# One fused transformer layer on one core: Gelu rebuilt from tanh tile by tile, a reordered prologue, zero products in TensorE's gaps, and a new step table

## The chip, the core and the metric

The kernel runs on one core of one Trainium2 chip. The core has five engines that run their own instruction lists side by side: TensorE (PE in the profile, with its weight loads as PEld), VectorE (DVE), ScalarE (ACT), GpSimd (POOL) and SyncE (SP, which here only issues transfers). They meet through semaphores. The metric is the device time of one execution in microseconds; lower is better. The time before is the median of three executions, 686.83 us (685.43 to 691.41).

## The reference

The input x has 2048 rows of 512 in bf16. It is layer-normalised, and the normalised rows feed two branches whose results are added to x:

```python
xn = _layernorm(x)
return x + A(xn, wqkv, wo) + B(xn, w1, b1, w2, b2)

# A: attention with 32 heads of 16
qkv = xn @ wqkv;  p = softmax(q k^T * 16 ** -0.5);  A = (p v) @ wo
# B: a second layernorm, then an MLP along the 2048 rows ("token mixing"), 1376 hidden
h = _layernorm(xn)
u = gelu(h^T @ w1 + b1)          # approximate=True, the tanh form; 512 x 1376
B = (u @ w2 + b2)^T
```

The tanh form of Gelu is 0.5 u (1 + tanh(0.798 (u + 0.0447 u^3))).

## The kernel before, in words

**The attention.** Scores are made transposed, 128 keys by 512 queries for one head: a *tile*. There are 32 heads x 16 key blocks x 4 query blocks = 2048 of them. They are worked off in 32 *blocks* of 4 heads x 16 key blocks, and `pos()` counts in blocks. Four heads' score products (`score_mm`, L621) run as four row strips of PE's array, each into one of seven PSUM banks. A bank is emptied in one of two ways:

- ACT takes the exponential (`exp_tile`, L634) of one, two or three neighbouring banks into the ring `pT`. One product with V (`pv_mm`, L647) uses each tile.
- DVE makes an approximate exponential with integers (`dve_first`, L667): the bits of an int16 read as bf16. Its error is evened out by two more copies, shifted by a constant, which POOL (an integer add, L676) or DVE (L678) makes four tiles at a time (`make_plane`). Three products with V then use each such tile. The copies live in `planes` and, once they are free, in `x_sb` and `xn_sb`.

The eighth bank gathers the product with V for one block; DVE copies it out (L1057), and the row sums go through DRAM and come back as factors for L1100.

**The MLP.** For each of 11 blocks of hidden columns, 16 product groups accumulate h^T w1 in a bank (`chain_ut`), DVE adds the bias into `gT` (L953), and after the eleventh block one call, `gelu_all`, runs Gelu on ACT: one instruction over ten blocks (L931), one over the last (L934). From then on 16 chains `chain_yo` make the products with w2, add wo's and the residual (`xres`) and store through `osb`. The hidden blocks are planned for positions 4.4 to 15.28 and the output chains from 15.68 on (`ut` and `yo` in L60).

**The order of work.** Nothing is ordered by the hardware: a planner in Python runs when the kernel is built. It keeps a clock for each engine, a cost for each operation and, for each engine in turn, picks the next instruction; each engine's list is then fixed, with waits where an operand comes from another engine. The engines run their lists in order. `pe_step` chooses among score products, PV products, a step of an MLP or projection chain, and, when nothing fits, `z_fill` (L1553): four products of zeros added to the PV bank. It does so until position 5 (`z_to`), and only where ACT has enough work queued. [...] `burst` chooses how many of the next four tiles go to DVE; the balance between ACT and DVE, the width of ACT's instructions and much else are parameters, and the table `STEP_VALUES` (L66) sets them anew at each of 32 positions.

**The prologue** (L457 to L716) is written out by hand. The loads: SP issues x tile 0, 1, 2, 3, then the weights of v, then the rest of x; ACT issues the first weights of q and k, and loads the table set that has both ln and exp. PE runs 8 zero products (L682), then for each of four tiles of x: statistics (DVE, L493), one over the deviation (two small ACT steps, L500 and L502), normalisation (DVE, L507), transpose (PE, L546), copy (ACT or DVE), projection to q (L534). Tile 0 of k follows, and after the fourth tile the first masked q (L587) and the first exponential.

Of the kernel before, what the change touches and what calls it, by code (L numbers as in the profile page):

```python
# [41 lines left out]
def _plane_sum(i):  # L42
    tot = 0.0
    for d, w in zip(SHIFT, WEIGHT):
# [10 lines left out]
N_ZERO0 = 8  # L55
N_ZERO1 = 2
NXP = 5
# [4 lines left out]
            pl_open=3, f_bias=0.0, f_early=9.0, s_wait=-1e9, tol2=-1e9, ex2=2.0, ex3=1.0, d_from=1.3, z_to=5.0, partial=False, pr_ex=0, dve_planes=6,  # L62
            v1=lambda a: (1.2 + 0.8 * a / 16.0, 0.6), v2=lambda a: (2.4 + 1.3 * a / 16.0, 1.6),
            kt=lambda T, c: ((0, 1.0, 2.9, 4.6)[T] + 0.17 * c * (1, 1, 2, 2)[T], (0, 0.5, 2.0, 3.2)[T]))
STEP_KEYS = ("bal", "bal_w", "d_from", "d_keep", "d_last", "d_slack", "d_stop", "dve_planes", "early", "ex2", "ex3", "f_bias", "f_early", "f_items", "f_late", "f_pr", "lk", "lone", "lone_n", "marg", "one_first", "open_pl", "partial", "pl_next", "pl_open", "pr_ex", "q_max", "ring_low", "ring_next", "tol", "trip")
STEP_VALUES = (  # L66
# [32 lines left out]
)  # L99
STEPS = [dict(zip(STEP_KEYS, v)) for v in STEP_VALUES]  # L100
HOOK = [None]
SCORE = (1.05, 0.5, 0.3)
CP_EVERY = 64
NU = 16
NQS = 4
NW1 = 2
NW2 = 2


# [1711 lines left out]
```

## Time and profile before

| | us |
|---|---|
| median of three executions | 686.83 |
| the profiled execution | 684.76 |
| its span, first to last instruction | 683.0 |
| ACT busy | 664.8 |
| PE busy (modelled ends) | 655.6 |
| DVE busy | 567.9 |
| POOL busy | 493.7 |
| first exponential starts | 12.97 |
| Gelu on ACT, with its two table loads | 341.04 to 348.64 |

Rows of groups read: line, engine, operation, out<-in, count, then busy us, mean ns of one, and the idle time of the engine just before them with what ended it. In a timeline row the first two numbers are start and length in us, and a bracket gives the idle time before. Windows give busy time for each engine, with the granted clock of PE (1.00 is full).

### The profile page before, as it was taken

To read this page: it belongs to the slowest core of one execution; us is meant where nothing else is said; L and a number is where in the kernel's file an instruction comes from. 1 tells how busy PE (TensorE), PEld (TensorE's weight loads), DVE (VectorE), ACT (ScalarE), POOL (GpSimd) and SP (SyncE) were. 2 spreads that over 40 slices of the span, in tenths; PEclk is the share of its full clock that TensorE was granted. 3 is DMA by queue.
4 is the path that set the end of the run, shared out by engine and by line. 5 is a ranking of instruction groups with operands and counts; after the bars stand their busy time and mean duration, and the time that the engine had idled before them with its cause. 6 is when DMAs were issued, how large, how long until landed. Compare 5 with 4: busy or idle time off the path is not lost.

```text
span 683.0 us, 20375 instructions
## 1 busy us (share of the span) xinstructions
PE 655.6 (96%) x8596; PEld 205.4 (30%) x8597; DVE 567.9 (83%) x939; ACT 664.8 (97%) x822; POOL 493.7 (72%) x515
## 2 busy tenths in 40 slices
PE   7899999999999999999989999999999999999996
PEld 3433333332222233323322222222323222222222
DVE  7888978779778798888958898788888899887794
ACT  5999999999999999999999999999999999999995
POOL 2409888767766679766678666669989699788783
PEclk9999999999999999999999999999999999999999
DMA  7050100112122021210021012121221211111101
GB/s 217 22 125 11 27 4 14 35 29 51 42 48 49 10 57 41 47 43 12 18 54 47 27 45 59 42 48 47 57 60 27 66 29 37 38 40 32 37 16 48
DMA packets 69957, 30.00 MB, mean 44 GB/s; under 512 B 56494, under 2 KB 66734, under 8 KB 69866
## 3 DMA queue, kind: packets, MB, share of 16 engines
q1 hardware_dynamic: 68522, 28.18, 16.7%
q8 instruction: 67, 1.10, 0.7%
q10 hardware_dynamic: 1344, 0.52, 0.3%
q14 instruction: 24, 0.20, 0.1%
HBM read 22.15 MB, written 2.61 MB: 36 GB/s over the span
## 4 chain that ended last, share of the span: by engine, by line
ACT 63%; PE 27%; DVE 5%; DMA 3%; issue 1%; SPq 0%; DVEq 0%; ACTq 0%
ACT pT L634 61%; PE ps L621 11%; PE ps L647 10%; PE ps L534 6%; DVE xn_sb L667 1%; DMA denb<-rec_scr 1%; DVE x_sb L667 1%; DMA rec_scr<-den 1%; ACT gT L931 1%; DMA x_sb<-in_A_x_dram 1%; DVE planes L667 0%; DVE xn_sb L507 0%; DVE oT L1100 0%; DVE stats L493 0%; DVE x_sb L678 0%
## 5 line engine op out<-in xcount | busy, mean ns | idle before, releaser
L634 ACT ACTIVATE pT<-ps 128x1024 bf16<-128x1024 f32 (+2 forms) x790 | 649.0, 1055 | 2.7 <-PE ps L621 2.3
L621 PE MATMUL ps<-QT,KT 32*128 32x512 bf16 x2048 | 274.2, 385 | 10.1 <-ACT pT L634 3.4
L667 DVE TENSOR_SCALAR planes<-ps 128x512 int16<-128x512 f32 x331 | 217.3, 684 | 43.4 <-PE ps L621 42.3
L647 PE MATMUL ps<-pT,V 128*32 128x512 bf16 x1397 | 225.7, 387 | 1.4 <-ACT pT L634 1.2
L667 DVE TENSOR_SCALAR x_sb<-ps 128x512 int16<-128x512 f32 x230 | 156.2, 685 | 32.6 <-PE ps L621 26.2
L621 PEld LDWEIGHTS ps<-QT,KT 32*128 32x128 bf16 x2048 | 76.7, 91 | 262.9 <-ACT pT L634 211.1
L676 POOL INT64_ADD planes<-planes x91 | 96.7, 1067 | 29.6 <-DVE planes L667 15.8
L647 PE MATMUL ps<-planes,V 128*32 128x512 bf16 x569 | 117.2, 385 | 0.0
L676 POOL INT64_ADD x_sb<-planes x82 | 88.9, 1089 | 30.8 <-PE ps L621 14.0
L676 POOL INT64_ADD planes<-x_sb x86 | 91.1, 1065 | 24.3 <-DVE x_sb L667 24.0
L647 PE MATMUL ps<-x_sb,V 128*32 128x512 bf16 x467 | 98.1, 385 | 0.0
L676 POOL INT64_ADD x_sb<-x_sb x60 | 63.4, 1061 | 40.3 <-DVE x_sb L667 36.6
L647 PE MATMUL ps<-planes,V17b 128*32 128x512 bf16 x331 | 83.7, 385 | 1.3 <-DVE OT L1057 1.3
L647 PEld LDWEIGHTS ps<-pT,V 128*32 128x32 bf16 x1397 | 55.6, 94 | 71.6 <-issue 59.6
L667 DVE TENSOR_SCALAR xn_sb<-ps 128x512 int16<-128x512 f32 x90 | 61.3, 686 | 11.9 <-PE ps L621 9.2
L676 POOL INT64_ADD xn_sb<-planes x48 | 51.7, 1081 | 15.3 <-DVE planes L667 15.3
L534 PE MATMUL ps<-gT,w2blk 128*32 128x512 bf16 (+1 forms) x704 | 59.6, 382 | 2.7 <-ACT gT L931 1.9
L647 PE MATMUL ps<-x_sb,V17b 128*32 128x512 bf16 x230 | 60.5, 386 | 0.6 <-DVE OT L1057 0.5
L534 PE MATMUL ps<-xn_sb,w1blk 128*32 128x512 bf16 x688 | 57.2, 381 | 0.0
L647 PE MATMUL ps<-xn_sb,V 128*32 128x512 bf16 x266 | 57.2, 385 | 0.0
L534 PE MATMUL ps<-xnT,wqkv_sb 128*32 128x512 bf16 (+3 forms) x624 | 44.6, 344 | 1.5 <-DVE xnT L559 1.1
L647 PEld LDWEIGHTS ps<-planes,V 128*32 128x32 bf16 x569 | 28.7, 95 | 18.5 <-issue 12.7
(91 smaller groups left out, 537.3 us busy)
## 6 DMA issues: line engine op xcount, KB each, us to landing
w1blk<-in_B_w_dram SPq DMA_DIRECT2D x10, 512.0 KB
w2blk<-in_B_w_dram SPq DMA_DIRECT2D x16, 320.0 KB, 3.4
denb<-rec_scr SPq DMA_DIRECT2D x16, 256.0 KB
xres<-in_A_x_dram SPq DMA_DIRECT2D x16, 128.0 KB, 2.9
QT<-qraw SPq DMA_DIRECT2D x120, 16.0 KB, 1.8
OT<-OT SPq DMA_DIRECT2D x60, 32.0 KB, 2.0
out_dram<-osb SPq DMA_DIRECT2D x13, 128.0 KB, 1.7
x_sb<-in_A_x_dram SPq DMA_DIRECT2D x2, 512.0 KB, 7.2
```

The source lines that it names most:

```text
L534: op = sc.add("pe", lambda e, sl=sl, c=c: e.matmul(dst[sl, :], lhsT=lhsT[:, sl], rhs=rhs, start=start, stop=stop, tile_position=(0, 32 * c ...
L621: return sc.add("pe", lambda e: e.matmul(bank(bk), lhsT=KT[32 * r:32 * r + 32, T, 128 * kt:128 * (kt + 1)], rhs=QT[32 * r:32 * r + 32, slo ...
L634: return sc.add("act", lambda e: e.activation(pick(pT, us), pick(ps3, bs), ACTF.Exp, scale=EXP_SCALE), reads=[("bank", b) for b in bs], wr ...
L647: return sc.add("pe", lambda e: e.matmul(bank(PV_BANK)[32 * r:32 * r + 32, :], lhsT=vt_[:, off:off + 32], rhs=rhs, start=start, stop=stop, ...
L667: return vec("dve", lambda e: e.tensor_scalar(plane_i[pb][:, 512 * r:512 * (r + 1)], bank(bk), BIAS + SHIFT[0], float(SHIFT[0]), ALU.add, ...
L676: return sc.add("pool", lambda e: e.int64_add(plane_q[pb], plane_q[pb0], -down * LANES), reads=rd, writes=wr, name="plane", occ=1015.0, la ...
L931: sc.add("act", lambda e: e.activation(gT[:, 0:NFTF, :], gT[:, 0:NFTF, :], ACTF.Gelu_apprx_tanh), reads=[("gT", f) for f in range(NFTF)], ...
```

## The change

**Gelu.** `gelu_all` goes. As soon as a hidden block is out of its bank, four steps follow it: the bias step now also halves the value (h = u / 2), then POOL squares h into a scratch tile (f32, the memory of `osb`), DVE makes (h^2 + 1 / (4 * 0.0447)) h into a second one (the memory of `xres`), ACT takes tanh with the constants in its scale, and DVE makes (tanh + 1) h in place. All 11 blocks share the two scratch tiles. The planner expects one table load at the first tanh.

**Loads and prologue.** ACT issues x tiles 2 and 3 in place of the weights of q and k; SP issues x tiles 0 and 1 and then the first weights of q, k and v. The masks (`const_q`) are made before the first statistics. The order on PE is now: transpose of a tile, then the projection of the one before, with the K projection behind the third tile's q; transpose 3 comes ahead of the projection of tile 2. Statistics of tile 4 are made after the masked q. There are 11 opening zero products, two behind the first transpose and two behind the first projection.

**Zero products.** `z_fill` works to the end, whenever fewer columns than `z_cols` were planned in the last 3.1 us; it can use a free score bank where the PV bank is not open, and the condition on ACT's queue is gone.

[...]

```diff
--- before.py
+++ after.py
@@ -52,55 +52,59 @@
 
 DEBUG_SCHED = False
 FORM = "P"
-N_ZERO0 = 8
+N_ZERO0 = 11
 N_ZERO1 = 2
+N_ZERO2 = 2
 NXP = 5
 DEBUG_CHAINS = False
 PLANNED = [0.0]
 TUNE0 = dict(bal=600.0, one_first=False, bal_w=2000.0, lk=0.1, trip=False, marg=60.0, q_max=1400.0, early=0.0, q_lead=0.72, ut=(4.4, 15.28), yo=(15.68, 30.47), d_keep=2, d_last=5, open_pl=2, d_stop=20, w3=1200.0,
             ring_low=4, tol=100.0, lone=800.0, lone_n=2, f_pr=2, f_late=0.2, f_items=3, ring_next=4, pl_next=4, d_slack=120.0,
-            pl_open=3, f_bias=0.0, f_early=9.0, s_wait=-1e9, tol2=-1e9, ex2=2.0, ex3=1.0, d_from=1.3, z_to=5.0, partial=False, pr_ex=0, dve_planes=6,
+            pl_open=3, f_bias=0.0, f_early=9.0, s_wait=-1e9, tol2=-1e9, ex2=2.0, ex3=1.0, d_from=1.3, z_cols=3500.0, partial=False, pr_ex=0, dve_planes=6,
             v1=lambda a: (1.2 + 0.8 * a / 16.0, 0.6), v2=lambda a: (2.4 + 1.3 * a / 16.0, 1.6),
             kt=lambda T, c: ((0, 1.0, 2.9, 4.6)[T] + 0.17 * c * (1, 1, 2, 2)[T], (0, 0.5, 2.0, 3.2)[T]))
-STEP_KEYS = ("bal", "bal_w", "d_from", "d_keep", "d_last", "d_slack", "d_stop", "dve_planes", "early", "ex2", "ex3", "f_bias", "f_early", "f_items", "f_late", "f_pr", "lk", "lone", "lone_n", "marg", "one_first", "open_pl", "partial", "pl_next", "pl_open", "pr_ex", "q_max", "ring_low", "ring_next", "tol", "trip")
+STEP_KEYS = ("bal", "bal_w", "d_from", "d_keep", "d_last", "d_slack", "d_stop", "dve_planes", "early", "ex2", "ex3", "f_bias", "f_early", "f_items", "f_late", "f_pr", "lk", "lone", "lone_n", "marg", "one_first", "open_pl", "partial", "pl_next", "pl_open", "pr_ex", "q_max", "ring_low", "ring_next", "tol", "trip", "z_cols")
 STEP_VALUES = (
-    (200.0, 2000.0, 1.0, 4, 4, 0, 0, 6, 200.0, 2.0, 1.0, 0.3, 0.2, 99, 0, 2, 0.2, 1500, 2, 60.0, True, 3, False, 5, 3, 0, 1000.0, 4, 10, 150.0, True),
...
+    (400.0, 2000.0, 1.2, 3, 4, 0, 10, 4, 100.0, 1.5, 1.0, 0, 9.0, 99, 0.4, 0.5, 0, 800, 2, 60.0, False, 1, True, 5, 3, 0, 1400.0, 3, 8, 100.0, False, 3500.0),
...
 )
 STEPS = [dict(zip(STEP_KEYS, v)) for v in STEP_VALUES]
 HOOK = [None]
 SCORE = (1.05, 0.5, 0.3)
 CP_EVERY = 64
+
+GE = "pool"
+GELU_C = 0.7978845608028654
 NU = 16
 NQS = 4
 NW1 = 2
@@ -148,6 +152,7 @@
         self.cfg = None
         self.port = 0.0
         self.cols = {}
+        self.recent = []
         self.busy = {e: 0.0 for e in self.ENGS}
 
     def ready(self, reads=(), writes=(), eng=None):
@@ -218,6 +223,9 @@
             k = int(t / TICK)
             share = 1.0 if cfg == "F" else 0.25
             self.cols[k] = self.cols.get(k, 0.0) + n * share
+            self.recent.append((t, n * share))
+            if len(self.recent) > 400:
+                del self.recent[:200]
             occ = (n / 2.4 * f + 10.0) if last else 4.0
             lat = n / 2.4 * f + 212.0
         op.start = t
@@ -403,7 +411,7 @@
             return sc.add(eng, fn, reads=reads, writes=writes, name=name, port=port, **t)
 
         def memset(eng, dst, v, writes, n=16, reads=()):
-            return sc.add(eng, lambda e: e.memset(dst, v), reads=reads, writes=writes, occ=max(50.0, n / 0.96), lat=max(50.0, n / 0.96) + 150.0)
+            return sc.add(eng, lambda e: e.memset(dst, v), reads=reads, writes=writes, occ=max(50.0, n / 0.96), lat=max(50.0, n / 0.96) + 150.0, port=eng == "pool" and n > 100)
 
 
         for j in range(32):
@@ -454,14 +462,14 @@
                 A_wqkv[:, c0:c1].rearrange("(ct p) n -> p ct n", p=128),
                 reads=[], writes=[("wqkv", j, T) for T in range(T0_, T1_)], name="ld_wqkv", lat=lat)
 
-        ld_x("sp", 0, 1, 2300)
-        ld_w("act", 0, 0, 1, 3300)
-        ld_x("sp", 1, 2, 2600)
-        ld_w("act", 1, 0, 1, 3600)
+        ld_x("sp", 0, 1, 3000)
+        ld_x("act", 2, 3, 4300)
+        ld_x("sp", 1, 2, 3000)
+        ld_x("act", 3, 4, 4200)
         sc.add("act", lambda e: e.preload_act_table_set("natural_log_exp_and_others"), occ=1300, lat=1300)
-        ld_x("sp", 2, 3, 2900)
-        ld_x("sp", 3, 4, 3200)
-        ld_w("sp", 2, 0, 1, 4000)
+        ld_w("sp", 0, 0, 1, 5000)
+        ld_w("sp", 1, 0, 1, 5000)
+        ld_w("sp", 2, 0, 1, 5200)
         ld_x("sp", 4, 6, 4000)
         ld_x("sp", 6, 8, 4500)
         ld_x("sp", 8, 12, 6000)
@@ -687,33 +695,44 @@
             for ct in range(NCT):
                 qt_mm(0, 0, ct, 4, 128 * t, 128)
 
+        def zeros(n):
+            for _ in range(n):
+                zero_mm(7)
+
+        const_q()
         ln_stats(0)
         ln_rstd(0, 1)
-        for t in range(4):
-            if t < 3:
-                ln_stats(t + 1)
-            ln_norm(t)
-            if t == 1:
-                const_q()
-                const_v(0, 1)
-            if t == 3:
-                ln_stats(4)
-            transpose_pe(t, TBK[t], 0)
-            if t > 0:
-                pro_q(t - 1)
-            if t == 2:
-                for ct in range(NCT):
-                    kt_mm(0, 0, 1, ct, 2)
-            for _ in range(N_ZERO1 if t < 3 else 0):
-                zero_mm(7)
-            if t < 3:
-                ln_rstd(t + 1, t + 2)
-            transpose_copy(t, 1, TBK[t], "act" if t < 3 else "dve")
-            if t == 2:
-                kt_evac(0, 0, 1, 2, "act")
+        ln_stats(1)
+        ln_norm(0)
+        transpose_pe(0, TBK[0], 0)
+        zeros(N_ZERO1)
+        ln_rstd(1, 2)
+        transpose_copy(0, 1, TBK[0], "act")
+        ln_stats(2)
+        ln_norm(1)
+        transpose_pe(1, TBK[1], 0)
+        const_v(0, 1)
+        pro_q(0)
+        zeros(N_ZERO2)
+        ln_rstd(2, 3)
+        transpose_copy(1, 1, TBK[1], "act")
+        ln_stats(3)
+        ln_norm(2)
+        transpose_pe(2, TBK[2], 0)
+        pro_q(1)
+        ln_rstd(3, 4)
+        transpose_copy(2, 1, TBK[2], "act")
+        ln_norm(3)
+        transpose_pe(3, TBK[3], 0)
+        pro_q(2)
+        for ct in range(NCT):
+            kt_mm(0, 0, 1, ct, 2)
+        transpose_copy(3, 1, TBK[3], "dve")
+        kt_evac(0, 0, 1, 2, "act")
         pro_q(3)
         qt_evac_masked(0, 0, 0, 4, "dve")
         qt_evac_masked(0, 0, 1, 4, "act")
+        ln_stats(4)
 
 
         TUNE = dict(TUNE0)
@@ -927,14 +946,35 @@
                 B_b2[128 * st:128 * (st + 1)].rearrange("(o p) -> o p", o=1),
                 reads=[], writes=[("w2blk", slot, 2)], name="ld_b2", lat=4500)
 
-        def gelu_all():
-            sc.add("act", lambda e: e.activation(gT[:, 0:NFTF, :], gT[:, 0:NFTF, :], ACTF.Gelu_apprx_tanh),
-                   reads=[("gT", f) for f in range(NFTF)], writes=[("gT", f) for f in range(NFTF)],
-                   occ=1300 + 512 * NFTF / 1.2 + 100, lat=1300 + 512 * NFTF / 1.2 + 300)
-            op = sc.add("act", lambda e: e.activation(gT[0:MLAST, NFTF, :], gT[0:MLAST, NFTF, :], ACTF.Gelu_apprx_tanh),
-                        reads=[("gT", NFTF)], writes=[("gT", NFTF)], occ=1300 + 512 / 1.2 + 100, lat=512 / 1.2 + 300)
-            gelu_done[0] = True
-            return op
+        gelu_left = [NFT]
+        GC = 4.0 * 0.044715
+        gA, gB = osb[:, :, :].rearrange("p a n -> p (a n)").bitcast(F32), xres[:, :, :].rearrange("p a n -> p (a n)").bitcast(F32)
+        kA, kB = [("osb", 0), ("osb", 1)], [("xres", 0), ("xres", 1)]
+
+        def gelu_steps(ft, m):
+            h = gT[0:m, ft, :]
+            n_ = 0 if ft else 1
+
+            def sq():
+                return sc.add(GE, lambda e: e.tensor_tensor(gA[0:m, :], h, h, ALU.mult), reads=[("gT", ft)], writes=kA,
+                              port=True, **(dict(occ=1300.0, lat=1450.0) if GE == "pool" else T_DVE(512)))
+
+            def cube():
+                return vec("dve", lambda e: e.scalar_tensor_tensor(gB[0:m, :], gA[0:m, :], 1.0 / GC, h, ALU.add, ALU.mult),
+                           [("gT", ft)] + kA, kB, 512, port=True)
+
+            def tanh():
+                t = T_ACT(512)
+                return sc.add("act", lambda e: e.activation(gB[0:m, :], gB[0:m, :], ACTF.Tanh, scale=2.0 * GELU_C * GC),
+                              reads=kB, writes=kB, occ=t["occ"] + 1300.0 * n_, lat=t["lat"] + 1300.0 * n_)
+
+            def mul():
+                op = vec("dve", lambda e: e.scalar_tensor_tensor(h, gB[0:m, :], 1.0, h, ALU.add, ALU.mult),
+                         [("gT", ft)] + kB, [("gT", ft)], 512, port=True)
+                gelu_left[0] -= 1
+                gelu_done[0] = gelu_left[0] == 0
+                return op
+            return [Step(GE, sq, 650), Step("dve", cube, 650), Step("act", tanh, 480), Step("dve", mul, 650)]
 
         def chain_ut(ft, due, rel):
             slot = ft % NW1
@@ -950,14 +990,13 @@
             ch.steps = [Step("pe", lambda st=st: mm(st), 226) for st in range(NT)]
 
             def ev():
-                op = vec("dve", lambda e: e.tensor_scalar(gT[0:m, ft, :], bank(ch.bk[0])[0:m, :], b1f[0:m, ft:ft + 1], None, ALU.add),
+                op = vec("dve", lambda e: e.tensor_scalar(gT[0:m, ft, :], bank(ch.bk[0])[0:m, :], b1f[0:m, ft:ft + 1], 0.5, ALU.add,
+                                                          ALU.mult),
                          [("bank", ch.bk[0]), ("b1f",)], [("gT", ft)], 565)
                 ut_done[0] += 1
-                if ut_done[0] == NFT:
-                    bg.append(Chain("gelu", [Step("act", gelu_all, 8000)], -5.0, 0.0, ex=False))
-                    bg[-1].t = op.end
                 return op
             ch.steps.append(Step("dve", ev, 650, frees=True))
+            ch.steps += gelu_steps(ft, m)
             return ch
 
         def yt_mm(ch, st, ft, first, last):
@@ -1406,6 +1445,11 @@
             for bs in groups:
                 us = ring_pick(len(bs), taken)
                 if us is None:
+                    us = ring_pick(2, taken) if len(bs) == 3 else None
+                    if us is not None:
+                        taken += us
+                        grp.append((bs[0:2], us))
+                        bs = bs[2:]
                     for k in bs:
                         us = ring_pick(1, taken)
                         taken += us
@@ -1546,22 +1590,29 @@
             if pvc and t_s is None and n_assigned[0] == 64 * NBLK:
                 pv_issue(pvc)
                 return True
-            if t + 226 + (SWITCH if sc.cfg != "P" else 0) <= min(lim, sc.free["act"] - 300.0):
+            if t + 226 + (SWITCH if sc.cfg != "P" else 0) <= lim:
                 return z_fill(t)
             return False
 
         def z_fill(t):
-            k = int(t / TICK)
-            if pos() >= TUNE["z_to"] or sc.cols.get(k, 0.0) >= TICK_COLS + 300.0 or not pv_open[0]:
-                return False
-            if sc.ready(writes=[("bank", PV_BANK)], eng="pe") > t:
+            if sum(n for v, n in sc.recent if v > t - TICK + 300.0) >= TUNE["z_cols"]:
                 return False
             b = pv_block[0]
-            for r in range(4):
-                sc.add("pe", lambda e, r=r, st=not started[b][r]: e.matmul(
-                    bank(PV_BANK)[32 * r:32 * r + 32, :], lhsT=zer[:, 512:544], rhs=zer[:, 0:512], start=st, stop=False,
-                    tile_position=(0, 32 * r)), reads=[("zer",)], writes=[("bank", PV_BANK)], cfg="P", n=512, last=r == 3)
-            started[b] = [True] * 4
+            rows = range(4)
+            if pv_open[0] and sc.ready(writes=[("bank", PV_BANK)], eng="pe") <= t:
+                rows = [r for r in range(4) if row_left[b][r] or items_left[b][r]]
+                bk, st, sp_ = PV_BANK, [not v for v in started[b]], False
+                for r in rows:
+                    started[b][r] = True
+            else:
+                fb = free_banks(t)
+                if not fb:
+                    return False
+                bk, st, sp_ = single_pick(fb), [True] * 4, True
+            for r in rows:
+                sc.add("pe", lambda e, r=r: e.matmul(
+                    bank(bk)[32 * r:32 * r + 32, :], lhsT=zer[:, 512:544], rhs=zer[:, 0:512], start=st[r], stop=sp_,
+                    tile_position=(0, 32 * r)), reads=[("zer",)], writes=[("bank", bk)], cfg="P", n=512, last=r == rows[-1])
             return True
 
         tail = dict(pre=0)
```

62 rows, old and new, of the table STEP_VALUES are left out of this document.

## The prediction

> **What bounds the kernel now.** I read the page's engine shares first, then the clock row and the chain that ended last.
>
> ```profile
> span 683.0 us, 20375 instructions
> ...
> PE 655.6 (96%) x8596; PEld 205.4 (30%) x8597; DVE 567.9 (83%) x939; ACT 664.8 (97%) x822; POOL 493.7 (72%) x515
> ...
> PEclk9999999999999999999999999999999999999999
> ...
> ACT 63%; PE 27%; DVE 5%; DMA 3%; issue 1%; SPq 0%; DVEq 0%; ACTq 0%
> ```
>
> ACT is busy 97% of 683.0 us; PE's 96% says little, since modelled matmul ends fill it. Next I read busy time by stage (columns: PE, PEld, DVE, ACT, POOL, granted clock, DMA share, GB/s) and the longest waits.
>
> ```profile
> 13.00:341.00 328.00, 318.28 (x4480) 107.14 (x4470) 276.45 (x467) 327.00 (x418) 223.49 (x216) 1.00 0.16 37
> 341.00:348.65 7.65, 5.73 (x100) 2.30 (x99) 1.92 (x4) 7.59 (x6) 4.08 (x4) 1.00 0.13 33
> 348.65:674.90 326.25, 318.75 (x3845) 90.49 (x3845) 275.69 (x427) 324.10 (x387) 262.20 (x250) 1.00 0.17 42
> ```
>
> ```profile
> PEld ps L621 <- ACT pT L634: 211.1, 509, 1.0
> ...
> DVE planes L667 <- PE ps L621: 42.3, 105, 6.0
> ```
>
> From 13 to 674.9 us ACT is idle for only 661.9 - (327.00 + 7.59 + 324.10) = 3.2 us, and PE's score loads wait 211.1 us for ACT to empty a bank. So the end is set by three numbers: when the first exponential starts, how much work ACT holds, and the tail behind its last exponential (674.9 to 683.0, untouched by the change). The middle is read from the groups:
>
> ```profile
> L634 ACT ACTIVATE pT<-ps 128x1024 bf16<-128x1024 f32 (+2 forms) x790 | 649.0, 1055 | 2.7 <-PE ps L621 2.3
> ...
> L667 DVE TENSOR_SCALAR planes<-ps 128x512 int16<-128x512 f32 x331 | 217.3, 684 | 43.4 <-PE ps L621 42.3
> L647 PE MATMUL ps<-pT,V 128*32 128x512 bf16 x1397 | 225.7, 387 | 1.4 <-ACT pT L634 1.2
> L667 DVE TENSOR_SCALAR x_sb<-ps 128x512 int16<-128x512 f32 x230 | 156.2, 685 | 32.6 <-PE ps L621 26.2
> ...
> L667 DVE TENSOR_SCALAR xn_sb<-ps 128x512 int16<-128x512 f32 x90 | 61.3, 686 | 11.9 <-PE ps L621 9.2
> ```
>
> ACT takes 1397 score tiles in 649.0 us, 0.465 us each; the vector path takes 331 + 230 + 90 = 651. Every tile that changes sides moves the end by 0.465 us. That is the exchange rate of this prediction. The profiled execution took 684.76 us (1.76 outside its span); the sum is made against it. The median of the three runs is 686.83, which is 2.07 more.
>
> **The change part by part.**
>
> *Prologue.* These rows show the start on SP's and ACT's queues, PE, DVE and ACT.
>
> ```profile
> 0.72 1.04 ACTq L398 DMA_DIRECT2D wqkv_sb<-in_A_wqkv_dram  x2
> ...
> 0.73 1.81 SPq L398 DMA_DIRECT2D x_sb<-in_A_x_dram  x4
> ...
> 1.24 3.60 PE L540 MATMUL ps<-zer 128*128 128x512 bf16 x8 [1.24 <-DVE zer L406]
> ...
> 4.06 0.69 DVE L493 BATCH_NORM_STATS2 stats<-x_sb 128x6 f32<-128x512 bf16 x1
> ...
> 5.33 0.43 PE L546 MATMUL ps<-ident,xn_sb 128*128 128x128 bf16 x4 [0.49 <-DVE xn_sb L507]
> ...
> 6.01 0.69 DVE L493 BATCH_NORM_STATS2 stats<-x_sb 128x6 f32<-128x512 bf16 x1 [0.74 <-DMA x_sb<-in_A_x_dram]
> 6.74 0.18 DVE L495 BATCH_NORM_AGGREGATE mv<-stats 128x2 f32<-128x6 f32 x1
> 6.84 0.38 DVE L507 TENSOR_SCALAR xn_sb<-x_sb,mv 128x512 bf16<-128x512 bf16 x1
> ...
> 7.16 0.40 DVE L406 MEMSET qmask<- 16x1 f32 x8
> ...
> 9.16 0.41 DVE L507 TENSOR_SCALAR xn_sb<-x_sb,mv 128x512 bf16<-128x512 bf16 x1 [0.37 <-ACT mv L502]
> ...
> 11.54 0.75 DVE L587 TENSOR_SCALAR QT<-ps,qmask 128x512 bf16<-128x512 f32 x1 [0.51 <-PE ps L534]
> ...
> 12.97 1.44 ACT L634 ACTIVATE pT<-ps 128x1536 bf16<-128x1536 f32 x1
> ```
>
> Tile 2 of x makes DVE wait 0.74 us; the mask memsets cost 0.40 us in the middle. With x tiles 2 and 3 first on ACT's queue and the masks before tile 0, DVE runs tile after tile: 0.91 us for a tile's statistics (6.01 to about 6.9) and 0.38 us for a normalisation. From the second tile at 4.06 that gives 4.06 + 3 x 0.91 + 3 x 0.38 = 7.9 us, and the last normalisation some 0.3 later, after its two small ACT steps: about 8.2 against 9.16, 1.0 us earlier. Tile 3's transpose now stands ahead of the third projection, not behind it and the K projection, which is worth about 0.4. Statistics of tile 4 leave the path. Together -1.4 us. Against it, the weights move behind x: those of q are now the third issue on SP, after two x issues of 1.81 / 4 = 0.45 us, so at about 1.64 instead of 0.72.
>
> ```profile
> DMA to landing us min/median/max: 4.2/6.2/8.0
> ```
>
> Landing 6.2 us later is 7.84, and PE wants them at about 7.3, after the second transpose; transposes 2 and 3 stand behind that projection in PE's list. At the maximum it is 9.64, 2.3 us late. I take 0.2 us of loss, as x no longer shares the first microseconds with weights: **-1.2 us, bounds -2.2 to +0.9**. Three more opening zero products at 3.60 / 8 = 0.45 us end near 6.2 us, after the first transpose's 5.33; PE's first transpose may slip by 0.9, but the later tiles are paced by DVE, so I count nothing (it is inside the upper bound).
>
> *Gelu on ACT.* ACT's timeline around it:
>
> ```profile
> 341.04 1.28 ACT L931 ACT_TABLE_LOAD   x1
> 342.33 4.47 ACT L931 ACTIVATE gT<-gT 128x5120 bf16<-128x5120 bf16 x1
> 346.71 0.61 ACT L934 ACTIVATE gT<-gT 96x512 bf16<-96x512 bf16 x1
> 347.35 1.28 ACT L634 ACT_TABLE_LOAD   x1
> 348.64 4.20 ACT L634 ACTIVATE pT<-ps 128x1024 bf16<-128x1024 f32 x4
> ```
>
> Removed: 348.64 - 341.04 = 7.60 us. Added: one load of 1.28 where tanh first appears (later exponentials are taken to stay in its set), and 11 tanh of 512 columns at 0.61 less an overlap of 0.09 (4.47 against 346.71 - 342.33 = 4.38), 0.52 each, 5.7 in all. **Net -0.6 us**; between -1.5 and +0.5 for a f32 operand, which no row shows here.
> [...]
>
> *The stall that goes.* While ACT is away, its banks stay full, PE issues no scores and DVE starves:
>
> ```profile
> 348.96 0.69 DVE L667 TENSOR_SCALAR planes<-ps 128x512 int16<-128x512 f32 x1 [6.04 <-PE ps L621]
> ```
>
> In 6.04 us DVE could evacuate 6.04 / 0.61 = 9.9 tiles (0.61 is about 0.685 less overlap), worth 9.9 x 0.465 = 4.6 us of ACT. PE used the gap for products that it needs anyway, so I take half: **-2.3 us, bounds -4.6 to 0**.
>
> *What the new Gelu costs elsewhere.* Per tile: a square on POOL, and on DVE two passes with two inputs in SBUF. DVE gets 22 such passes. Two rows bracket one:
>
> ```profile
> L1100 DVE TENSOR_TENSOR oT<-OT,denb 128x512 bf16<-128x512 f32 x16 | 15.2, 951 | 6.6 <-DMA denb<-rec_scr 6.6
> ...
> L1016 DVE TENSOR_TENSOR osb<-ps,xres 128x512 bf16<-128x512 f32 x12 | 8.2, 681 | 0.1
> ```
>
> L1100 has both inputs in SBUF, so 22 x 0.951 = 20.9 us (15.0 at 0.681). They fall into the stage of the W1 products:
>
> ```profile
> 134.60:340.50 205.90, 201.69 (x2475) 61.24 (x2472) 173.97 (x272) 205.89 (x260) 143.91 (x135) 1.00 0.17 38
> ```
>
> DVE is idle 205.9 - 174.0 = 31.9 us there and POOL 62.0. Nothing waits for the Gelu itself: its readers start after position 15, and the scratch tiles osb and xres are first needed then. But behind each DVE pass stand evacuations, and their banks come free late. Bounds: nothing, if the idle time takes all 20.9 us; 20.9 / 0.61 = 34 tiles, 15.9 us, if it takes none. DVE's waits for scores are short (42.3 us in 105), too short for a whole pass, but a backlog is worked off in the next gap. I take a quarter, nearest to the bound that the 31.9 us support: **+4.0 us**. POOL's 11 squares, at the 1.07 us of the integer add below or twice that, are 12 to 24 us in 62.0 idle: nothing, unless a tanh is queued on ACT before its square and cube are done. All exponentials stand behind it then; one us each would be 11 us. ACT's 2.3 us of waits for PE say that such planned orders hold on the chip, so I count nothing.
>
> ```profile
> L676 POOL INT64_ADD planes<-planes x91 | 96.7, 1067 | 29.6 <-DVE planes L667 15.8 <-PE ps L621 12.8 <-issue 0.5
> ```
>
> [...]
>
> *Zero products and the new step table.* The clock is granted at 1.00 in every stage above, so zero products can speed up nothing that this trace shows. What they alter is the plan: the planner books PE at half speed after any thin interval, which the clock row shows nowhere, and orders work by that. With the gaps filled on paper it sees PE free, and each tile on the vector path needs one score and three PV products. The table's 32 rows are chosen anew for it, so the split 1397 / 651 changes, and this no row can price. Groups of three also split into two and one, not three ones; that saves some instructions. Bounds: 20 tiles either way (3% of 651), +9.3 to -9.3 us. DVE's total idle, 683.0 - 567.9 = 115.1 us, leaves more room upward than down: I take 8 tiles, **-3.7 us**. A zero product that delays a score is covered by the 211.1 us that PE waits for ACT anyway.
>
> Sum: 684.76 - 1.2 - 0.6 - 2.3 + 4.0 - 3.7 = **681.0 us**, 0.8% under the median.
>
> **The rivals.**
> - *The room is used in full.* The 31.9 us hide all DVE passes, the whole stall comes back, 20 tiles move: 684.76 - 1.2 - 0.6 - 4.6 - 9.3 = 669.1. For it: DVE at 83%. Against: its gaps are short.
> - *The plan gains nothing.* 684.76 - 1.2 - 0.6 - 2.3 + 4.0 = 684.7. For it: ACT is full before and after, and nothing in the rows forces a better split.
> - *DVE becomes the bound in the W1 stage* (the other side). Its 174.0 + 20.9 us are 95% of 205.9; if its gaps are structural, 34 tiles go back to ACT, and the new table wins none: 684.76 - 1.2 - 0.6 - 2.3 + 15.9 = 696.6. It decides from about 19 tiles lost (+9 us, by which the time passes the median); the 105 waits speak for it, the 31.9 us against.
> - *The set isn't shared*: every tanh brings a load, and one back: 21 loads more than the one counted, 21 x 1.28 = 26.9, so 707.9. The rows show only that ACT went from one set to another and back. [...]
>
> **How the numbers follow.** Forecast 681.0, itself good for 675 to 686: 0.43. Room in full 0.20, plan gains nothing 0.17, DVE the bound 0.17, sets not shared 0.03. A difference of 1% (6.9 us) is about what a measurement of this kernel can tell from no change: the three runs lie from 685.43 to 691.41. Faster by more, under 680.0: all of the second case and some 0.20 of the first, 0.40. Slower by more, over 693.7: 0.16 of the fourth, the fifth, and a sliver: 0.20. The rest, 0.40, is within 1%. The range 668 to 697 leaves out the set case, the lower part of the full-room case and the upper part of the DVE case, together under 0.2.
>
> **What would show it.** First exponential near 11.7 instead of 12.97; two table loads instead of three, none near 341; eleven tanh with no idle time before them; DVE passes near 0.95 us; ACT's tile count (the PV products from pT) near 1389; clock 1.00 as before. I am wrong if that count rises by more than 15, if ACT waits for DVE before its tanh, or if the first exponential comes later than 13.

## The result and the profile after

The changed kernel takes 820.79 us (819.23 to 822.36, 4 runs); the kernel before takes 686.67. The ratio is 1.194, with a 95% interval of 1.188 to 1.200. The forecast was 681.0, its range ended at 697, and even its slowest rival said 707.9.

The page of the changed kernel, the rows that answer to those of before:

```profile
span 819.2 us, 20399 instructions
...
PE 693.7 (85%) x8579; PEld 204.2 (25%) x8579; DVE 564.9 (69%) x934; ACT 671.6 (82%) x835; POOL 499.0 (61%) x529
...
PEclk9999999788697797896976969999999999999999
...
PE 50%; ACT 22%; issue 12%; DVE 10%; POOL 4%; DMA 1%; DVEq 0%; POOLq 0%; ACTq 0%
...
L642 ACT ACTIVATE pT<-ps 128x1024 bf16<-128x1024 f32 (+2 forms) x795 | 656.2, 1018 | 79.8 <-PE ps L629 78.9
...
L655 PE MATMUL ps<-pT,V 128*32 128x512 bf16 x1401 | 232.5, 401 | 1.0 <-DVE V L567 1.0
...
L959 POOL TENSOR_TENSOR osb<-gT 128x512 f32<-128x512 bf16 (+1 forms) x11 | 11.3, 1031 | 79.2 <-issue 79.2
```

ACT and POOL have little more work than before, ACT 671.6 us against 664.8 and POOL 499.0 against 493.7, and ACT holds 1401 tiles, 4 more. PE is busy for 693.7 us against 655.6, but with no more products (8579 against 8596): in the stretch of the lower clock they are longer. A score product takes 416 ns on the mean from 134 to 482 us, at a clock of 0.81, 384 ahead of it and 387 behind it; over the whole span that makes 396 against 385. What is new is idle time on ACT, which was hardly ever idle, and a clock row that sinks in one stretch. The chain now runs over PE and has 12% of "issue", time in which an engine waited for nothing that the profile can name. The last row holds the key: POOL sat idle for 79.2 us before 11 squares, and nothing released it.

POOL's timeline of the changed kernel around the first square:

```profile
135.55 2.06 POOL L684 INT64_ADD planes<-planes  x2 [1.14 <-DVE planes L675]
145.18 1.03 POOL L959 TENSOR_TENSOR osb<-gT 128x512 f32<-128x512 bf16 x1 [7.58 <-issue]
152.18 1.03 POOL L684 INT64_ADD x_sb<-planes  x1 [5.97 <-issue]
```

The square itself takes 1.03 us. Ahead of it stand 7.58 us of nothing, and behind it 5.97 more before the next integer add. What POOL's queue holds there stands among the instructions of the two lines; first L959 and L684 of the changed kernel, then L676, the integer add of the kernel before:

```profile
L959 POOLq MODIFY_POOL_CONFIG  x22: 4/11/12, 137.6 to 468.2; - x22
...
  issue: 79.2, 11
```

```profile
L684 POOLq MODIFY_POOL_CONFIG  x24: 1/1/1, 30.2 to 476.2; - x24
...
  issue: 59.3, 10
```

```profile
L676 POOLq MODIFY_POOL_CONFIG  x2: 1/1/1, 31.8 to 31.8; - x2
```

The build puts a pair of these in front of the square and another in front of the next integer add: 22 and 24 in the changed kernel, where the kernel before has 2 in all, at 31.8 us, inside 20 us in which POOL had nothing to do. The 11 pauses ahead of squares are 7.2 us each (79.2 / 11), those named behind them 5.9 (59.3 / 10); the eleventh, 5.75 us, is put down to a DVE instruction.

Who pays is in the longest waits of the changed kernel (engine and tile, what ended the wait, us in total, times, longest):

```profile
POOL osb L959 <- issue: 79.2, 11, 7.6
ACT pT L642 <- PE ps L629: 78.9, 44, 7.8
DVE xres L963 <- POOL osb L959: 68.2, 11, 7.8
DVE planes L675 <- PE ps L629: 62.1, 127, 6.4
...
ACT xres L968 <- DVE xres L963: 53.6, 11, 6.1
PEld ps L655 <- POOL x_sb L684: 47.9, 14, 12.5
...
PEld ps L655 <- POOL planes L684: 39.2, 25, 12.8
```

One pause goes two ways. Through the Gelu: DVE's cube waits for the square with evacuations behind it (68.2 us), ACT's tanh waits for the cube with exponentials behind it (53.6 us). Through the planes: POOL's integer adds come late, and PE, whose list is fixed, waits for one up to 12.8 us.

### The profile page after: what moved, and what is told of

The parts are those of the page before. It is cut to its first block, busy times and chain, and to the rows that moved or that the text cites. A ratio compares the mean times of both kernels' runs of the same rounds, so it can differ in the third digit from the quotient of the medians.

```text
span 819.2 us, 20399 instructions
## 1 busy us (share of the span) xinstructions
PE 693.7 (85%) x8579; PEld 204.2 (25%) x8579; DVE 564.9 (69%) x934; ACT 671.6 (82%) x835; POOL 499.0 (61%) x529
## 4 chain that ended last, share of the span: by engine, by line
PE 50%; ACT 22%; issue 12%; DVE 10%; POOL 4%; DMA 1%; DVEq 0%; POOLq 0%; ACTq 0%
ACT pT L642 22%; PE ps L655 19%; PE ps L629 19%; PE ps L542 12%; DVE planes L675 3%; DVE x_sb L675 2%; POOL osb L959 1%; POOL planes L684 1%; POOL x_sb L684 1%; DVE xres L963 1%; DVE xn_sb L515 1%; PE ps L1613 1%; DMA denb<-rec_scr 1%; DVE stats L501 0%; DVE gT L993 0%
## 5 line engine op out<-in xcount | busy, mean ns | idle before, releaser
L642 ACT ACTIVATE pT<-ps 128x1024 bf16<-128x1024 f32 (+2 forms) x795 | 656.2, 1018 | 79.8 <-PE ps L629 78.9
L629 PE MATMUL ps<-QT,KT 32*128 32x512 bf16 x2048 | 288.8, 396 | 15.5 <-DVE planes L675 6.3
L675 DVE TENSOR_SCALAR planes<-ps 128x512 int16<-128x512 f32 x313 | 208.1, 686 | 63.2 <-PE ps L629 62.1
L675 DVE TENSOR_SCALAR x_sb<-ps 128x512 int16<-128x512 f32 x211 | 144.3, 687 | 62.3 <-PE ps L629 57.8
L684 POOL INT64_ADD planes<-planes x93 | 97.0, 1047 | 52.3 <-issue 23.7
L684 POOL INT64_ADD x_sb<-planes x90 | 94.4, 1054 | 37.5 <-issue 17.8
L684 POOL INT64_ADD planes<-x_sb x78 | 81.8, 1054 | 33.6 <-DVE x_sb L675 20.9
L675 DVE TENSOR_SCALAR xn_sb<-ps 128x512 int16<-128x512 f32 x123 | 84.0, 687 | 22.6 <-PE ps L629 19.8
L655 PE MATMUL ps<-planes,V17b 128*32 128x512 bf16 x313 | 84.3, 406 | 13.0 <-DVE OT L1096 12.8
L684 POOL INT64_ADD x_sb<-x_sb x57 | 59.4, 1045 | 43.6 <-DVE x_sb L675 30.6
L655 PEld LDWEIGHTS ps<-pT,V 128*32 128x32 bf16 x1401 | 55.3, 95 | 67.6 <-issue 59.3
L542 PE MATMUL ps<-xn_sb,w1blk 128*32 128x512 bf16 x688 | 67.4, 416 | 0.0
L959 POOL TENSOR_TENSOR osb<-gT 128x512 f32<-128x512 bf16 (+1 forms) x11 | 11.3, 1031 | 79.2 <-issue 79.2
L963 DVE SCALAR_TENSOR_TENSOR xres<-osb,gT 128x512 f32<-128x512 f32 (+1 forms) x11 | 7.6, 692 | 68.2 <-POOL osb L959 68.2
L968 ACT ACTIVATE xres<-xres 128x512 f32<-128x512 f32 (+1 forms) x11 | 6.9, 629 | 53.6 <-DVE xres L963 53.6
```

The costliest lines, as they stand in the source:

```text
L542: op = sc.add("pe", lambda e, sl=sl, c=c: e.matmul(dst[sl, :], lhsT=lhsT[:, sl], rhs=rhs, start=start, stop=stop, tile_position=(0, 32 * c ...
L629: return sc.add("pe", lambda e: e.matmul(bank(bk), lhsT=KT[32 * r:32 * r + 32, T, 128 * kt:128 * (kt + 1)], rhs=QT[32 * r:32 * r + 32, slo ...
L642: return sc.add("act", lambda e: e.activation(pick(pT, us), pick(ps3, bs), ACTF.Exp, scale=EXP_SCALE), reads=[("bank", b) for b in bs], wr ...
L655: return sc.add("pe", lambda e: e.matmul(bank(PV_BANK)[32 * r:32 * r + 32, :], lhsT=vt_[:, off:off + 32], rhs=rhs, start=start, stop=stop, ...
L675: return vec("dve", lambda e: e.tensor_scalar(plane_i[pb][:, 512 * r:512 * (r + 1)], bank(bk), BIAS + SHIFT[0], float(SHIFT[0]), ALU.add, ...
L684: return sc.add("pool", lambda e: e.int64_add(plane_q[pb], plane_q[pb0], -down * LANES), reads=rd, writes=wr, name="plane", occ=1015.0, la ...
```

## The experiments

*The theory after the traces (A):* each square makes POOL change its code (what the configuration pair is taken to stand for) and back, and since four lists are fixed in one order, everything waits. *Rivals:* DVE has become the bound (B, the prediction's own slow rival); the new order and table are at fault (C).

**e1, the squares on DVE.**

```diff
-GE = "pool"
+GE = "dve"
```

> The changed kernel with the 11 squares on DVE in place of POOL; all else as changed, planned anew. Theory A (each square makes POOL change its code, about 7.2 us before it and 5.9 us before the next integer add, and everything waits): no pause is left, so 675 to 695 us, clock 1.00, ACT's waits for PE under 10 us in all. Rival B (DVE has become the bound): DVE has 11 passes more than in the changed kernel, so 820 or more. Rival C (the new order and table are at fault): 780 to 830, as the order is much the same.

706.28 us, ratio 1.0225 (1.0176 to 1.0274). B falls: with 11 DVE passes more the kernel is 114.5 us faster than with squares on POOL. But 706 lies above A's 675 to 695; something of 16 us is left over the kernel before. The tile counts point to what; the exponentials' products in e1 and ACT's waits:

```profile
L655 PE MATMUL ps<-pT,V 128*32 128x512 bf16 x1430 | 229.6, 387 | 1.0 <-DVE V L567 1.0
```

```profile
ACT pT L642 <- PE ps L629: 7.2, 7, 2.8
```

1430 tiles on ACT, 33 more than before: 33 x 0.465 = 15.3 us. ACT hardly waits; it has more to do, because the planner, with the table of another program, moved fewer tiles to DVE. That is an argument so far (the table's *misfit* below); e9 tests it.

**e2, the old Gelu in the changed kernel.**

```diff
...
+                if ut_done[0] == NFT:
+                    bg.append(Chain("gelu", [Step("act", gelu_all, 8000)], -5.0, 0.0, ex=False))
...
-            ch.steps += gelu_steps(ft, m)
```

> The changed kernel with the old Gelu (one call on ACT after the eleventh block); new prologue, zero products, step table and planner stay. Theory A: 675 to 695 us. Rival C (order and table): 780 to 830. Rival B: 675 to 695 as well, since DVE has no added passes; e1 tells A from B.

701.81 us, ratio 1.0157 (1.0098 to 1.0217): far below C's 780, so the loss sits in the Gelu. Again above A's range, with 1428 tiles on ACT:

```profile
L642 ACT ACTIVATE pT<-ps 128x1024 bf16<-128x1024 f32 (+1 forms) x847 | 665.9, 1055 | 3.5 <-PE ps L629 2.9
...
L655 PE MATMUL ps<-pT,V 128*32 128x512 bf16 x1428 | 225.0, 388 | 1.5 <-DVE V L567 1.0 <-ACT pT L642 0.2
```

**e3, three squares on POOL, eight on DVE.**

```diff
+            ge = "pool" if ft in (1, 4, 7) else "dve"
...
-                return sc.add(GE, lambda e: e.tensor_tensor(...
+                return sc.add(ge, lambda e: e.tensor_tensor(...
...
```

> The changed kernel with 3 of the 11 squares (blocks 1, 4, 7) on POOL and 8 on DVE. Theory A: three times two code changes, each pair about (820.8 - e1) / 11 = 12 us, so 36 us over e1, about 720. Rival B or C: within 15 us of e1.

750.15 us in its one run, 43.9 over e1, where A said 36 and B and C at most 15. Its plan has 9 tiles more on ACT than e1 (1439), 4.2 us; the rest is 39.7 / 3 = 13.2 us for a square. POOL's pauses are there three times each, first those behind the squares, then those ahead of them, 13.0 us for a pair ((17.6 + 21.3) / 3):

```profile
L684 POOLq MODIFY_POOL_CONFIG  x8: 1/1/1, 30.7 to 327.0; - x8
...
  issue: 17.6, 3
```

```profile
L960 POOLq MODIFY_POOL_CONFIG  x6: 7/11/11, 157.0 to 318.9; - x6
...
  issue: 21.3, 3
```

The price goes by the number of squares.

**e4, POOL memsets in the kernel before.**

```diff
                 ut_done[0] += 1
+                if ft in range(11):
+                    memset("pool", osb[:, 0, 0:16], 0.0, [("osb", 0)])
```

> The kernel before with one memset of 16 columns of osb on POOL added behind each of the 11 bias steps; nothing computes with it. Theory A, if the code change comes with any ordinary POOL instruction between integer adds: 11 pairs of 13 us on POOL, and PE and ACT stall for the late planes: 760 to 830 us. If a memset needs no change, or POOL's idle 30% hides it: 685 to 700. Rival B and C: 685 to 700.

689.68 us in its one run, within the spread of the kernel before beside it (686.17 to 693.63). POOL's timeline, where one memset stands between integer adds, and the configuration row of its integer adds:

```profile
151.87 2.05 POOL L676 INT64_ADD planes<-x_sb  x2 [3.51 <-DVE x_sb L667]
153.86 0.11 POOL L406 MEMSET osb<- 128x16 bf16 x1
156.91 2.05 POOL L676 INT64_ADD planes<-x_sb  x2 [2.94 <-DVE x_sb L667]
```

```profile
L676 POOLq MODIFY_POOL_CONFIG  x2: 1/1/1, 31.0 to 31.0; - x2
```

No pause, and no pairs but the two instructions that the kernel before has too. So theory A does not hold for any ordinary instruction between integer adds: a memset brings no change, the square does. This gives the test that decides.

**e5, the same order with a copy in the square's place.** The whole changed kernel, its plan untouched; the square is left out.

```diff
-                return sc.add(GE, lambda e: e.tensor_tensor(gA[0:m, :], h, h, ALU.mult), ...
+                return sc.add(GE, lambda e: e.tensor_copy(gA[0:m, :], h), ...
```

> The changed kernel, instruction for instruction in the same order, but POOL copies h into the scratch tile where it squared it (the square is left out, so the Gelu is another function). A copy brought no change of POOL's code when built, as the memsets of e4 did not. Theory A: the whole of the loss goes, 680 to 690 us, ACT waits for PE under 10 us, and what is left against the kernel before is the worth of the rest of the change: 1401 tiles on ACT against 1397 (+1.9), first exponential 1.6 earlier, Gelu -0.6, so about -0.3 to the 686.7 of before. Rival (a POOL step in the middle of DVE's and ACT's lists costs by itself, whatever its code): 750 or more.

685.15 us (683.99 to 688.01, 12 runs), ratio to the kernel before 0.9952 (0.9927 to 0.9978). One instruction, eleven times, is the whole loss of 135.6 us: 12.3 for a square. The two stages beside each other, each about as many instructions (PE 2508 and 2465, POOL 145 and 145); first the changed kernel, then e5 (columns as in the prediction):

```profile
134.00:482.00 348.00, 238.43 (x2508) 59.93 (x2501) 176.44 (x272) 220.94 (x259) 148.91 (x145) 0.81 0.10 23
```

```profile
134.00:345.00 211.00, 208.73 (x2465) 57.85 (x2457) 174.98 (x266) 210.97 (x254) 151.00 (x145) 1.00 0.16 37
```

348 us against 211, 137 more, about the 79.2 + 59.3 = 138.5 us of POOL's named pauses. In e5 the copy stands right behind an integer add, the pairs around the squares are gone with the pauses, and ACT waits for PE 2.1 us in all:

```profile
135.78 1.04 POOL L684 INT64_ADD planes<-planes  x1
136.76 0.61 POOL L959 CAST osb<-gT 128x512 f32<-128x512 bf16 x1
```

```profile
L684 POOLq MODIFY_POOL_CONFIG  x2: 1/1/1, 30.0 to 30.1; - x2
```

```profile
ACT pT L642 <- PE ps L629: 2.1, 5, 1.0
```

The copy takes 0.72 us on the mean, the square 1.03, so e5 is kinder to POOL by some 3 us of its idle time; that is not separated here.

**e6, short zero products in e5's order.**

```diff
+            zn = [512 if st[r] and not sp_ else 16 for r in range(4)]
...
-                    bank(bk)[32 * r:32 * r + 32, :], ..., rhs=zer[:, 0:512], ...
+                    bank(bk)[32 * r:32 * r + 32, 0:zn[r]], ..., rhs=zer[:, 0:zn[r]], ...
```

> e5 with its zero products cut from 512 to 16 columns, except those that open an accumulation; the order is that of e5. If zero products do nothing for the clock: within 2 us of e5, clock 0.99 or more in both. If they hold the clock up: windows with less than 1.00 and 5 us or more over e5.

685.39 us against 685.15, ratios 0.9953 and 0.9952, mean clock 1.00 in both. The zero products' columns are worth nothing in this order.

**e7, the new Gelu alone in the kernel before.**

```diff
...
-                if ut_done[0] == NFT:
-                    bg.append(Chain("gelu", [Step("act", gelu_all, 8000)], -5.0, 0.0, ex=False))
...
+            ch.steps += gelu_steps(ft, m)
```

> The kernel before with the new Gelu alone (squares on POOL), planned anew with the old step table. Theory A: 11 pairs of code changes, some 12 us each, and a table that no longer fits (as in e1, some 15): 815 to 840 us. If prologue, zero products or table are needed for the loss: under 750.

835.65 us in its one run, as A said. The loss needs neither prologue nor table nor zero products.

**e8, the prologue alone in the kernel before.**

```diff
-        ld_w("act", 0, 0, 1, 3300)
+        ld_x("act", 2, 3, 4300)
...
+        const_q()
         ln_stats(0)
         ln_rstd(0, 1)
-        for t in range(4):
...
+        ln_stats(1)
+        ln_norm(0)
...
```

> The kernel before with the new loads and prologue alone. First exponential at 11.4 us instead of 13.0, as in the changed kernel. If the step table fits only the program it was chosen for (e1 and e2 lost some 32 tiles to ACT): 695 to 705 us. If not: 685.

714.88 us, ratio 1.0352 (1.0299 to 1.0406): worse than even the misfit was said to be. The first exponential does start at 11.50 instead of 12.97:

```profile
11.50 1.44 ACT L635 ACTIVATE pT<-ps 128x1536 bf16<-128x1536 f32 x1
```

But the plan put 1447 tiles on ACT, 50 more, worth 23 us:

```profile
L648 PE MATMUL ps<-pT,V 128*32 128x512 bf16 x1447 | 237.0, 390 | 1.7 <-ACT pT L635 1.3
```

So an edit that gains 1.5 us at the front goes with a plan that costs fifteen times that. This was the last thing to settle: is it the fit of the table, or do the parts cost something?

**e9 and e10, a step table chosen anew for e1 and for e2.** Only `STEP_VALUES` differs from e1 and e2, by a search over the plan.

> e1 (squares on DVE) with a step table chosen anew for that program: 1406 tiles on ACT in 801 instructions, where e1 had 1430 in 835 and the kernel before 1397 in 790. If the 16 us that e1 lost were the table's fit alone: from the kernel before, 9 tiles x 0.434 + 11 instructions x 0.054 - 1.6 (first exponential) - 0.6 (Gelu) = +2.3, so 689 against 686.7, and under 692 in any case. If squares on DVE cost 10 us or more by themselves: over 697.

687.94 us, ratio 0.9987 (0.9955 to 1.0020), where e1 had 706.28. The 0.434 and 0.054 agree with ACT's exponentials before: one of three tiles took 1.591 us on the mean and one of two 1.157, 0.434 less; 649.0 - 1397 x 0.434 = 42.7 us are left for 790 instructions, 0.054 each.

> e2 (old Gelu, all else as changed) with a step table chosen anew for that program: 1405 tiles on ACT in 747 instructions, e2 had 1428 in 847. Table's fit alone: 8 x 0.434 - 43 x 0.054 - 1.6 = -0.4 against the kernel before, so 684 to 688. If prologue or zero products cost something by themselves: over 692.

684.25 us, ratio 0.9944 (0.9914 to 0.9974), where e2 had 701.81. What e1 and e2 had lost was the table's misfit; e8 was not run with a table of its own. ACT's exponentials in e9 and in e10:

```profile
L642 ACT ACTIVATE pT<-ps 128x1024 bf16<-128x1024 f32 (+2 forms) x801 | 655.3, 1062 | 6.4 <-PE ps L629 6.1
```

```profile
L642 ACT ACTIVATE pT<-ps 128x1024 bf16<-128x1024 f32 (+2 forms) x747 | 649.1, 1139 | 4.5 <-PE ps L629 4.3
```

Tiles are only a part of it. From e2 to e10, 23 tiles leave ACT (1405 against 1428), 10.7 us by 0.465; but the exponentials also come in 747 instructions instead of 847, and together their busy time falls by 16.8 us (665.9 to 649.1).

e10, with the old Gelu, the new prologue and its own table, is 0.6% faster than the kernel before and 136.5 us faster than the changed one; its median is the lowest measured. The tile-wise Gelu with its square on DVE (e9) can't be told from the kernel before, and beside e10 it is 3.7 us slower: no run here shows the new Gelu to gain anything over the old one. The two have different tables, so what those 3.7 us are is not shown.

## Why the prediction was wrong

**The step that failed** is the sentence that costs POOL's 11 squares at "12 to 24 us in 62.0 idle: nothing". It took the integer add's 1.07 us for the square's price, and that was even right: 1.03 us. What it left out is the change of kind: 7.2 us before the square and 5.9 after it, some 13 us of POOL a time, and 12.3 us of the end (e5). Eleven of them fill 143 us of POOL in a stage that had 62 idle, so the cover would have been gone even if nothing had waited at once. The trace of before held a hint: two configuration instructions on POOL's queue at 31.8, where the first integer adds follow on memsets, hidden by 20 us without work:

```profile
30.81 0.94 POOL L406 MEMSET wo_pad<- 128x1024 bf16 x1
52.01 1.04 POOL L676 INT64_ADD x_sb<-x_sb  x1 [20.26 <-DVE x_sb L667]
```

I read POOL's busy time and not its queue. The hint says that such a change exists, not which instructions bring it; that took e4 and e5.

The sentence's own exception ("unless a tanh is queued on ACT before its square and cube are done") names one of the two ways in which the pause spreads, but bounds it by one us each; ACT's waits for the cube came to 53.6 us in 11, one of the prediction's own signs of being wrong. The argument that ACT's 2.3 us of waits showed planned orders to hold was no argument for an instruction that the plan had never held.

What POOL does in the pauses is not shown. The traces have the configuration pairs, some 7.2 us of idle time ahead of a square and 5.9 behind it; that POOL changes its code there is my reading of them.

**Point by point, by e5** (the changed kernel without the pauses):

- *ACT is the bound, 0.465 us for a tile:* held. The misfits of e1, e2 and e8 follow roughly from their tile counts: 33, 31 and 50 tiles more, 15.3, 14.4 and 23.2 us, less what the prologue gains; measured 16.2, 11.7 and 26.1 over the medians of before beside them. e8 is some 4 us over its count, with 5.3 us of ACT's waits for PE.
- *Prologue -1.2:* right in sign and somewhat small. The first exponential starts at 11.39 instead of 12.97 (-1.6). The last normalisation came at 8.12 where 8.2 was worked out, and no instruction of PE waited for the weights. The rows of the changed kernel:

```profile
8.12 0.41 DVE L515 TENSOR_SCALAR xn_sb<-x_sb,mv 128x512 bf16<-128x512 bf16 x1 [0.49 <-ACT mv L510]
...
11.39 2.91 ACT L642 ACTIVATE pT<-ps 128x1024 bf16<-128x1024 f32 x4
```

- *Gelu on ACT -0.6:* held. There are two table loads instead of three, one at the start and one at the first tanh; the other ten tanh and the exponentials between them bring none, so that rival falls (its chance of 0.03 was my estimate, which no row of before shows). The load at the first tanh, from ACT's timeline of e5, has no gap behind it, and from the tanh's start to the next exponential's it is 0.54 us, where 0.52 was worked out:

```profile
140.39 1.28 ACT L968 ACT_TABLE_LOAD   x1
141.68 0.63 ACT L968 ACTIVATE xres<-xres 128x512 f32<-128x512 f32 x1
142.22 2.41 ACT L642 ACTIVATE pT<-ps 128x512 bf16<-128x512 f32 x3
```

- *The stall, the DVE passes and the new plan* (-2.3 + 4.0 - 3.7 = -2.0) can only be seen together, as tiles: 4 more on ACT, +1.9 us, where the sum had about 4 fewer (the sign that I named, 1389, took the new plan's 8 alone). The 22 DVE passes themselves took 19.1 us in e5, where I had 20.9. The plan did not use the room, and DVE did not become the bound; the truth lay near the rival "the plan gains nothing", 684.7, which is where e5 came out.
- *Zero products do nothing:* held for their columns where PE is fed (e6). The sentence that the clock stays at 1.00 fell with the pauses: 0.81 in that stage, where PE's products took 238.43 us against 208.73 in e5. Whether the low clock cost anything beside the pauses was not tried: the pauses alone come to the whole loss of that stage.
- *The slow rival* named DVE. Its place (the W1 stage) was right, its mechanism wrong.

## What to carry to other kernels

The price of a square on POOL had two parts here, its own 1.03 us and 13.1 of pauses around it (7.2 and 5.9); before giving POOL a new kind of work between instructions of another, look at its queue's configuration records in the old trace at the one place where the kind changes. With the lists fixed, idle share was no cover for the pauses: on an engine that had been 28% idle they kept PE waiting for up to 12.8 us at a time, and ACT and DVE for up to 7.8. And where a planner's parameters were chosen for one program, count the work on the bounding engine before blaming an edit: with a new table alone, 24 tiles came back from ACT in e9 and 23 in e10.

## What the runs showed of the hardware

- POOL between an integer add and a tensor-tensor product: 7.2 us on the mean (7.6 at most) ahead of the product, 5.9 back (6.1 at most), 11 times alike in the changed kernel; a memset (e4) or a copy (e5) in such a place brought none, with 2 configuration instructions in all instead of 46.
- Where a DVE pass with two SBUF inputs met an integer add of POOL in the kernel before, one of the two or both took longer. Of the 16 passes of L1100, the four with no integer add beside them took 0.68 us each, and the eleven that began while POOL was at an integer add 0.77 to 1.45. The one at 377.33 began ahead of an add and took 0.68; the add, begun at 377.52, took 1.40, where the median add takes 1.04. The cube took 0.692 us on the mean in the changed kernel, where POOL had just paused and no integer add fell beside it, and 0.844 in e5, where the median of all eleven is 0.685 and the longest 1.591. The groups of the changed kernel and of e5:

```profile
L963 DVE SCALAR_TENSOR_TENSOR xres<-osb,gT 128x512 f32<-128x512 f32 x10 | 6.9, 692 | 63.2 <-POOL osb L959 63.2
```

```profile
L963 DVE SCALAR_TENSOR_TENSOR xres<-osb,gT 128x512 f32<-128x512 f32 x10 | 8.4, 844 | 0.6 <-POOL osb L959 0.6
```

- PE's granted clock fell to 0.81 in a stage where PE waited for POOL up to 12.8 us at a time (the changed kernel, 134 to 482 us), and was 1.00 in the same work without the pauses (e5, 134 to 345 us).
